# Loading q, k and v of six batches as fp32 through the hardware queue, with the cast on GpSimd or VectorE, and transposing one more batch of x by DMA

## The chip, the cores and the metric

The kernel runs on one core of a Trainium2 chip. A core has TensorE (PE, matrix multiplication; its weight loads are shown as PEld), VectorE (DVE), ScalarE (ACT), GpSimd (POOL) and SyncE (SP, which here only issues transfers), each with a program of its own that it works through in order. Engines wait for one another through semaphores. DMA engines, 16 for the core, move data between HBM and the core's memory; transfers are issued by SyncE or ScalarE (the hardware queues) or by GpSimd (the software queue). A transfer from GpSimd may change the type of the data on the way[...].

The metric is the time of one execution on the device in microseconds, the median of several runs. The profile comes from one profiled execution; its span, from the first to the last instruction, is about 2 us shorter than the time.

## What is computed

Attention with a relative position bias for 8 batches of 8 heads, 576 positions and a head size of 64, and behind it a feed-forward layer with a squared relu on all 4608 rows:

```python
batch, n_heads, seq, head_dim = (8, 8, 576, 64)          # q, k, v in fp32
scores = scale * np.matmul(q, k.transpose(0, 1, 3, 2))
bias = bias_table[bucket]                                # depends on |i - j| only
scores = scores + bias.transpose(2, 0, 1)[None, :, :, :]
attn = np.exp(scores - np.max(scores, axis=-1, keepdims=True))
attn = attn / (np.sum(attn, axis=-1, keepdims=True) + 1e-09)
attn_out = np.matmul(attn, v)

x = attn_out.transpose(0, 2, 1, 3).reshape(B * S, H * D)  # 4608 x 512
h = np.maximum(x @ w_in, 0.0)                             # w_in  512 x 2048
out = h * h @ w_out                                       # w_out 2048 x 512, out in fp32
```

## The kernel before

Everything is computed in fp16 with sums in fp32. The kernel describes its work as operations with an estimated length, the buffers they hold, what they depend on and when they are due. A planner in the program sorts them into an order for every engine; the chip then runs these fixed orders. Constants such as `LEAD`, `PERIOD`, `G0` and `GP` set when attention and the layers are due, and so shape the order. They are no times of the chip.

The heads are worked on in pairs, four pairs per batch, 32 in all:

```python
DT_QK = 3
PERIOD, LEAD, FAST, FASTN = 9000.0, 9900.0, 4500, 6
AHEAD, G0, GP = 9800.0, 30900.0, 41900.0
DT_X = 2
RELU_DVE = 0
NSTG, NQK, NPT, NV, NX, NGB, NRT, NY = 2, 4, 2, 3, 2, 2, 4, 3   # buffers of each kind
SIX = 3
ORDER = "i0 i1 q0 k1 k0 i2 q1 o0 i3 v o1 o2 o3"                 # loads of w_in, w_out, batch 1
```

Loading. All loads of q, k, v and the weights are issued by GpSimd, in a fixed order, and turn fp32 into fp16 on the way. Batches 0 to 2 (`b < SIX`) lay q and k out in six positions per row, the others in plain rows of 64 elements:

```python
def load_six(b, w, h0, nh):
    l = load("POOL", nc.gpsimd,
        lambda: six(stg[b_stg[b].slot][w])[:, h0 : h0 + nh, :],
        const(src[b, h0 : h0 + nh].rearrange("h (p j) d -> p h (j d)", j=6)), ...)

def load_qk(b, w):                       # batches 3 to 7: ten transfers for q, ten for k
    tails = [load("POOL", nc.gpsimd, ...) for e in range(2)]
    for hp in range(4):
        l_qk[b, w, hp] = tails + [load("POOL", nc.gpsimd, ...) for e in range(2)]

def load_v(b):                           # four transfers of 128 rows, two for the last 64
    for tt in range(4):
        l = load("POOL", nc.gpsimd,
            lambda tt=tt: vas[b_v[b].slot][:, tt, :, 0:64],
            const(v[b, :, ts(tt, 128), :].transpose([1, 0, 2])), ...)
    load_v_tail(b)
```

Attention of a pair. q and k are transposed, by TensorE for batches 0 to 2 and by DMA from SyncE for the others (`b >= DT_QK`), asked for 6 us ahead of the scores. The last 64 positions of the two heads are copied into a small zeroed tile (`spread`). Scores (`L622`) use half of TensorE's rows for each head. Exponentials follow on ScalarE (`L633`, `L656`, `L681`), products with the bias factors on VectorE (`L714`), multiplication with v on TensorE (`L752`, `L759`), and division by the row sum on VectorE (`L776`, `L781`). The last two steps are done in two halves that share one PSUM buffer:

```python
if b >= DT_QK:
    nc.sync.dma_start_transpose(out=dst[qb.slot]..., in_=rows(stg[...][w])[:, hp]...)
elif b < SIX:                            # L577: 12 small transposes of 96 rows each
    for j in range(6):
        for e in range(2):
            nc.tensor.transpose(ps[ds(64 * e, 64), ts(j, 96)], six(t)[:, 2 * hp + e, ts(j, D)], id_sb[0:96, 0:96])
else:                                    # 5 transposes of 128 columns
    for j in range(5):
        nc.tensor.transpose(ps[:, ts(j, 128)], rows(t)[:, hp, j, :], id_sb)

def sp(o, ...):                          # L604, on VectorE or GpSimd
    eng.tensor_copy(out=dst[qb.slot][rw, rw], in_=src[qb.slot][rw, 512:576])

for part, qt0, nq in ((0, 0, 3), (1, 3, 2)):
    bank = Buf(r_pv)                     # one PSUM buffer
    ...                                  # L752, L759, then L776 and L781 on VectorE
    if b >= DT_X:                        # x transposed by DMA (L797), else by TensorE (L819)
        nc.sync.dma_start_transpose(out=xt_sb[:, hp, c : c + 128 * nq]..., in_=xs[xb.slot][...]...)
```

The layers. `xt_sb` is a ring for four batches of x (`XB = 4`, 2304 columns). The 4608 rows are done in nine groups of 512. Group g's first layer (`L914`, 16 blocks of 128 outputs, 4 matmuls each) is laid beside group g-1's second layer (`L864`). A group that runs over the end of the ring takes two matmuls in place of one:

```python
n = min(GT, XR - c)
for a, z, c in ((0, n, c), (n, GT, 0)):
    for kk in range(4 if z > a else 0):
        nc.tensor.matmul(g_ps[bank.slot][:, a:z], w_in_sb[:, kk, ts(nt, 128)], xt_sb[:, kk, c : c + z - a], ...)
...
engs = {"ACT": act(512), "DVE": dve(512)} if g < RELU_DVE else {"ACT": act(512)}   # L935, relu
nc.vector.tensor_tensor(out=gs[gb1.slot][:, nt, :], in0=rts[rb.slot], in1=rts[rb.slot], op=MULT)   # L945
```

Of the kernel before, what the change touches and what calls it, by code (L numbers as in the profile page):

```python
# [10 lines left out]
FP32 = mybir.dt.float32  # L11
FP16 = mybir.dt.float16
# [5 lines left out]
B, H, S, D = 8, 8, 576, 64  # L18
# [6 lines left out]
VW = 66  # L25
GT = 512
NG = B * S // GT
XB = 4
XR = XB * S
DT_QK = 3  # L30
PERIOD, LEAD, FAST, FASTN = 9000.0, 9900.0, 4500, 6
AHEAD, G0, GP = 9800.0, 30900.0, 41900.0
DT_X = 2
RELU_DVE = 0
NSTG, NQK, NPT, NV, NX, NGB, NRT, NY = 2, 4, 2, 3, 2, 2, 4, 3
SIX = 3
ORDER = "i0 i1 q0 k1 k0 i2 q1 o0 i3 v o1 o2 o3"


def _bucket(n):  # L40
# [140 lines left out]
def kernel(  # L181
# [10 lines left out]
    nc = tc.nc  # L192
    assert (_bucket(np.arange(128, S)) == NBK - 1).all()

    def io(ins):
        tc.keep_in_program_order(ins)
        return ins
# [10 lines left out]
    def sb(name, shape, dtype=FP16):  # L208
        return single.tile(shape, dtype, name=name)
# [3 lines left out]
    w_out_sb = sb("w_out_sb", [128, 16, 512])  # L213
# [8 lines left out]
    stg = [[sb(f"{n}s{i}", [128, 6 * 512]) for n in "qk"] for i in range(NSTG)]  # L222
# [7 lines left out]
    vas = [sb(f"va{i}", [128, 4, H, VW]) for i in range(NV)]  # L230
    v4s = [sb(f"vm{i}", [128, 4, 2, VW]) for i in range(NV)]
    xs = [sb(f"x{i}", [128, 4, 5, 128]) for i in range(NX)]
    xt_sb = sb("xt", [128, 4, XR + 64])
    gs = [sb(f"g{i}", [128, 16, GT]) for i in range(NGB)]
    rts = [sb(f"rt{i}", [128, GT]) for i in range(NRT)]
    ys = [sb(f"y{i}", [128, 512], FP32) for i in range(NY)]
    rs = [sb(f"r{i}", [128, 3, 2, 1], FP32) for i in range(2)]
# [4 lines left out]

    P = Plan()
    r_set, r_pv, r_g, r_lane = Ring(2), Ring(1), Ring(3), Ring(8)
    r_stg, r_qk, r_pt, r_v, r_x = Ring(NSTG), Ring(NQK), Ring(NPT), Ring(NV), Ring(NX)
    r_gb, r_rt, r_y, r_r = Ring(NGB), Ring(NRT), Ring(NY), Ring(2)

# [14 lines left out]
    def one_of(engs, fn, deps, bufs, due):  # L262
        op = P.add(engs, None, deps, bufs, due)
        op.fn = lambda: fn(op)
        return op

    def const(f):
        return lambda: f

    def load(eng_name, eng, out_, in_, packets, deps=(), bufs=(), due=0.0):  # L270
        return loader(eng_name, eng, out_, in_, packets, deps, bufs, due)[0]
# [30 lines left out]
        for i in range(4)  # L302
# [11 lines left out]
                out=eb_sb, in0=sel_sb, in1=ex_sb.rearrange("p (a h) -> p a h", a=1).to_broadcast([128, 4, 8]), op=MULT  # L314
# [43 lines left out]
    first, z_fix = [], []  # L358
# [37 lines left out]
    l_qk = {}  # L396
# [3 lines left out]
    def pdue():  # L400
        pool_due[0] += 1.0
        return pool_due[0]
# [5 lines left out]
    def rows(t):  # L408
        return t[:, 0:2560].rearrange("p (c t d) -> p c t d", c=4, t=5)

    def load_six(b, w, h0, nh):
        src = (q, k)[w]
        l = load(
            "POOL", nc.gpsimd,
            lambda: six(stg[b_stg[b].slot][w])[:, h0 : h0 + nh, :],
            const(src[b, h0 : h0 + nh].rearrange("h (p j) d -> p h (j d)", j=6)),
            96 * nh * 75, (), [b_stg[b]], pdue(),
        )
        for hp in range(h0 // 2, (h0 + nh) // 2):
            l_qk[b, w, hp] = [l]  # L420

    def load_qk(b, w):
        src = (q, k)[w]
        tails = [
            load(
                "POOL", nc.gpsimd,
                lambda e=e: rows(stg[b_stg[b].slot][w])[0:64, :, 4, ds(64 * e, D)],
                const(src[b, e::2, 512:S, :].transpose([1, 0, 2])),
                256 * 34.5, first, [b_stg[b]], pdue(),
            )  # L430
            for e in range(2)
        ]
        for hp in range(4):
            l_qk[b, w, hp] = tails + [
                load(
                    "POOL", nc.gpsimd,
                    lambda hp=hp, e=e: rows(stg[b_stg[b].slot][w])[:, hp, 0:4, ds(64 * e, D)],
                    const(src[b, 2 * hp + e, 0:512, :].rearrange("(t p) d -> p t d", p=128)),
                    512 * 34.5, first, [b_stg[b]], pdue(),
                )  # L440
                for e in range(2)
            ]

    def load_v_head(b, h):
        l = load(
# [16 lines left out]
                l_v.setdefault((b, hp), []).append(l)  # L462

    def load_v(b):
        for tt in range(4):
            l = load(
                "POOL", nc.gpsimd,
                lambda tt=tt: vas[b_v[b].slot][:, tt, :, 0:64],
                const(v[b, :, ts(tt, 128), :].transpose([1, 0, 2])),
                1024 * 34.5, v_all, [b_v[b]], pdue(),  # L470
            )
            for hp in range(4):
                l_v.setdefault((b, hp), []).append(l)
        load_v_tail(b)
# [34 lines left out]
    for step in ORDER.split():  # L509
        if step[0] == "i":  # L510
            load_w_in(int(step[1]))
        elif step[0] == "o":
            load_w_out(int(step[1]))
        elif step[0] in "qk":
            load_six(1, "qk".index(step[0]), 4 * int(step[1]), 4)
        else:
            load_v(1)
    for b in range(2, B):
        for w in range(2):
            if b < SIX:  # L520
                load_six(b, w, 0, 8)
            else:
                load_qk(b, w)
        load_v(b)


# [478 lines left out]
```

The softmax here doesn't subtract the row's maximum and nothing guards it: scores larger than these inputs give would overflow.

## Time and profile before

| | |
|---|---|
| time, median of 3 runs | 388.77 us (388.37 to 389.11) |
| span of the profiled execution | 386.6 us |
| TensorE busy | 370.2 us |
| ScalarE busy | 261.0 us |
| VectorE busy | 202.6 us |
| GpSimd busy, with the making of descriptors | 151.5 us |
| packets of the software queue | 94,432, 59.8% of 16 engines' span |
| packets of the hardware queue | 49,488, 24.2% of 16 engines' span |
| granted clock of TensorE | full throughout |

How to read it: a group's line gives the busy time of its instructions together, their mean length, and behind a second bar the idle time of their engine just before them with what ended it. Lengths of matmuls overlap, as they are pipelined; where the cost of one counts, the distance from one start to the next is what to take. The chain that ended last follows the run back from its last instruction, at each step to what released it. A share of the DMA engines over 1 in a stretch means that packets overlapped.

### The profile page before, as it was taken

To read this page: it belongs to the slowest core of one execution; us is meant where nothing else is said; L and a number is where in the kernel's file an instruction comes from. 1 tells how busy PE (TensorE), PEld (TensorE's weight loads), DVE (VectorE), ACT (ScalarE), POOL (GpSimd) and SP (SyncE) were. 2 spreads that over 40 slices of the span, in tenths; PEclk is the share of its full clock that TensorE was granted. 3 is DMA by queue.
4 is the path that set the end of the run, shared out by engine and by line. 5 is a ranking of instruction groups with operands and counts; after the bars stand their busy time and mean duration, and the time that the engine had idled before them with its cause. 6 is when DMAs were issued, how large, how long until landed. Compare 5 with 4: busy or idle time off the path is not lost.

```text
span 386.6 us, 8896 instructions
## 1 busy us (share of the span) xinstructions
PE 370.2 (96%) x3544; PEld 200.4 (52%) x3544; DVE 202.6 (52%) x526; ACT 261.0 (68%) x372; POOL 151.5 (39%) x260
## 2 busy tenths in 40 slices
PE   2779999999999999999999999999999999999996
PEld 2547455754445545454567665455544545444444
DVE  5889664856644654466545464545456442432200
ACT  2798986979766885689676675857478652654421
POOL 8884720595527364725338452835420000000000
PEclk9999999999999999999999999999999999999999
DMA  7999996499769598989989799799950112001012
GB/s 101 151 194 192 147 192 67 53 109 143 81 115 115 95 127 116 134 104 113 97 126 90 82 114 171 84 87 131 163 88 27 36 66 80 27 0 49 35 54 83
DMA packets 144201, 39.04 MB, mean 101 GB/s; under 512 B 130592, under 2 KB 139680, under 8 KB 144160
## 3 DMA queue, kind: packets, MB, share of 16 engines
q0 software_dynamic: 94432, 18.36, 59.8%
q1 hardware_dynamic: 49488, 19.98, 24.2%
q8 instruction: 28, 0.46, 0.5%
q10 hardware_dynamic: 240, 0.13, 0.2%
q14 instruction: 13, 0.11, 0.1%
HBM read 36.87 MB, written 9.44 MB: 120 GB/s over the span
## 4 chain that ended last, share of the span: by engine, by line
PE 89%; DMA 4%; ACT 3%; DVE 2%; issue 1%; SPq 0%; ACTq 0%; DVEq 0%
PE f L914 33%; PE f L864 30%; PE pv L759 9%; PE st L622 8%; PE pv L752 3%; PE st L671 2%; PE f L577 2%; PE st L646 2%; ACT pt L633 2%; DMA kt<-ks 1%; DMA xt<-x 1%; DMA far_sb<-in_bias_table_dram 1%; PE f L819 1%; ACT pt L656 0%; DVE pt L714 0%
## 5 line engine op out<-in xcount | busy, mean ns | idle before, releaser
L633 ACT ACTIVATE pt<-st 128x1024 f16<-128x1024 f32 x128 | 126.8, 1022 | 36.9 <-PE st L622 36.8
L864 PE MATMUL f<-w_out_sb,g 128*128 128x512 f16 (+1 forms) x592 | 141.0, 373 | 0.0
L914 PE MATMUL f<-xt,w_in_sb 128*128 128x512 f16 (+1 forms) x640 | 140.4, 358 | 0.1
L935 ACT ACTIVATE rt<-f 128x512 f16<-128x512 f32 x144 | 85.5, 598 | 48.5 <-PE f L914 47.2
L945 DVE TENSOR_TENSOR g<-rt 128x512 f16<-128x512 f16 x144 | 60.8, 422 | 66.6 <-ACT rt L935 65.8
L914 PEld LDWEIGHTS <-w_in_sb 128*128 128x128 f16 x640 | 59.1, 98 | 62.0 <-issue 10.6
L864 PEld LDWEIGHTS <-g 128*128 128x128 f16 x592 | 54.7, 98 | 57.7 <-issue 5.9
L714 DVE TENSOR_TENSOR pt<-pt,tb_sb 128x512 f16<-128x512 f16 (+2 forms) x96 | 59.0, 623 | 26.9 <-ACT pt L633 26.7
L759 PE MATMUL pv<-va,pt 128*128 128x65 f16 x1280 | 54.6, 193 | 0.0
L759 PEld LDWEIGHTS <-pt 128*128 128x128 f16 x1280 | 50.2, 97 | 4.3 <-issue 0.3
L604 POOL COPY qz<-qt 64x64 f16<-64x64 f16 x44 | 12.6, 286 | 85.7 <-DMA qt<-qs 56.9
L255 POOL DMA_DIRECT2D qs<-in_q_dram x57 | 40.8, 729 | 5.2 <-PE f L914 2.3
L622 PE MATMUL st<-qt,kt 64*128 64x512 f16 x256 | 40.1, 385 | 2.8 <-ACT pt L633 1.2
L255 POOL DMA_DIRECT2D ks<-in_k_dram x57 | 40.9, 747 | 1.8 <-issue 1.1
L752 PE MATMUL pv<-vm,pm 128*128 128x130 f16 x160 | 35.4, 221 | 0.3 <-DVE x L781 0.3
L781 DVE TENSOR_TENSOR x<-pv,r 128x384 f16<-128x384 f32 x64 | 31.4, 490 | 1.8
L255 POOL DMA_DIRECT2D va<-in_v_dram x36 | 30.8, 872 | 0.7 <-DMA ks<-in_k_dram 0.4
L776 DVE RECIPROCAL r<-pv 128x6 f32<-128x6 f32 x64 | 11.9, 187 | 36.0 <-PE pv L759 35.9
L604 POOL COPY kz<-kt 64x64 f16<-64x64 f16 x38 | 12.4, 327 | 39.7 <-DMA kt<-ks 35.9
L884 ACT ACTIVATE y<-f 128x512 f32<-128x512 f32 (+1 forms) x19 | 11.0, 578 | 21.0 <-PE f L864 20.8
L681 ACT ACTIVATE pm<-st 128x576 f16<-128x576 f32 x32 | 20.9, 652 | 4.2 <-PE st L671 4.0
L656 ACT ACTIVATE pt<-st 128x512 f16<-128x512 f32 x32 | 19.2, 600 | 3.6 <-PE st L646 3.4
(49 smaller groups left out, 174.7 us busy)
## 6 DMA issues: line engine op xcount, KB each, us to landing
out_dram<-y SPq DMA_DIRECT2D x35, 256.0 KB, 2.3
va<-in_v_dram POOLq DMA_DIRECT2D x28, 128.0 KB, 5.6
qs<-in_q_dram POOLq DMA_DIRECT2D x40, 64.0 KB, 3.1
ks<-in_k_dram POOLq DMA_DIRECT2D x40, 64.0 KB, 3.3
w_in_sb<-in_moe_w_in_dram POOLq DMA_DIRECT2D x4, 512.0 KB, 9.6
w_out_sb<-in_moe_w_out_dram POOLq DMA_DIRECT2D x4, 512.0 KB, 8.4
xt<-x SPq DMA_TRANSPOSE x48, 3.2
qs<-in_q_dram POOLq DMA_DIRECT2D x4, 144.0 KB, 4.8
```

The source lines that it names most:

```text
L255: lambda: io(eng.dma_start(out=out_(), in_=in_())),
L604: io(eng.tensor_copy(out=dst[qb.slot][rw, rw], in_=src[qb.slot][rw, 512:576]))
L622: nc.tensor.matmul(sets_ps[st.slot][:, e, :], kt[rw, ts(jt, 128)], qt[rw, 0:512], start=True, stop=True,)
L633: nc.scalar.activation(out=p5(pts[pb.slot])[:, jt, :, 0:512], in_=sets_ps[st.slot], func=EXPF, scale=SCALE)
L714: io(nc.vector.tensor_tensor(out=a, in0=a, in1=t, op=MULT))
L752: nc.tensor.matmul(ps[:, i, :, :], pm[:, c : c + 128], vm[:, hp, :, 0:65], start=True, stop=False)
L759: nc.tensor.matmul(ps[:, i, e, :], pt[:, (2 * jt + e) * S + c : (2 * jt + e) * S + c + 128], va[:, jt, 2 * hp + e, 0:65], start=False, sto ...
L781: nc.vector.tensor_tensor(out=xs[xb.slot][:, hp, qt0 : qt0 + nq, :].rearrange("p t (e d) -> p t e d", e=2), in0=ps[:, :, :, 0:64], in1=rs[ ...
L864: nc.tensor.matmul(g_ps[bank.slot][:, 0:cn], gs[gb.slot][:, nt, ts(m, 128)], w_out_sb[:, nt, c0 : c0 + cn], start=(nt == 0), stop=(nt == 15),)
L914: nc.tensor.matmul(g_ps[bank.slot][:, a:z], w_in_sb[:, kk, ts(nt, 128)], xt_sb[:, kk, c : c + z - a], start=(kk == 0), stop=(kk == 3),)
L935: io(nc.scalar.activation(out=rts[rb.slot], in_=g_ps[bank.slot], func=RELUF))
L945: nc.vector.tensor_tensor(out=gs[gb1.slot][:, nt, :], in0=rts[rb.slot], in1=rts[rb.slot], op=MULT)
```

## The change

q, k and v of batches 2 to 7 no longer come through GpSimd's transfers. SyncE loads tiles of 128 rows and 8 heads as fp32 into six buffers, and GpSimd or VectorE, whichever the planner picks, casts each into its place. The first of these loads is held back by a tiny transfer that reads w_out's second block, and so waits for it: batch 2 is not to take bandwidth from the weights. That frees GpSimd of most of its descriptors. Batch 2 now has plain rows (`SIX = 2`), so its q and k are transposed in five pieces. x of batch 1 is transposed by DMA (`DT_X = 1`). To make room for the buffers, the ring of x holds three batches. For the first three groups the relu may run on VectorE, the order of the first loads is another, and the constants of the planner are set anew.

```diff
-XB = 4
+XB = 3
-PERIOD, LEAD, FAST, FASTN = 9000.0, 9900.0, 4500, 6
-AHEAD, G0, GP = 9800.0, 30900.0, 41900.0
-DT_X = 2
-RELU_DVE = 0
+PERIOD, LEAD, FAST, FASTN = 8700.0, 4200.0, 4500, 6
+AHEAD, G0, GP = 7800.0, 24000.0, 41200.0
+DT_X = 1
+RELU_DVE = 3
-SIX = 3
-ORDER = "i0 i1 q0 k1 k0 i2 q1 o0 i3 v o1 o2 o3"
+NF = 6
+FOLLOW = 1
+SIX = 2
+ORDER = "i0 k0 q0 i1 q1 i2 k1 v o0 o1 i3 o2 o3"
...
+    fs = [sb(f"f32{i}", [128, 512], FP32) for i in range(NF)]
...
+    def through(src, put, n, w, dst_buf, engs, deps):
+        fb = Buf(r_f)
+        f32 = lambda: fs[fb.slot].rearrange("p (h d) -> p h d", d=D)
+        deps0 = []
+        if not started:
+            deps0 = [P.add({"SP": 430.0}, lambda: io(nc.sync.dma_start(
+                out=fs[fb.slot][0:1, 0:8].bitcast(FP16), in_=w_out_sb[0:1, 4 * FOLLOW + 3, 0:16])),
+                [l_wout[FOLLOW]], [fb], pdue())]
+            ...
+        issue = P.add({"SP": 430.0}, lambda: io(nc.sync.dma_start(out=f32()[n], in_=src)), deps0, [fb], pdue())
+        t = P.add({"DMA": w * 22.2 / 16}, None, [issue], [fb], pool_due[0])
+        def cast(o):
+            for out_, in_ in put(f32()):
+                io((nc.vector if o.eng == "DVE" else nc.gpsimd).tensor_copy(out=out_, in_=in_))
+        return one_of(engs, cast, [t] + list(deps), [fb, dst_buf], pool_due[0])
...
     def load_qk(b, w):
-        tails = [load("POOL", nc.gpsimd, ...) for e in range(2)]
+        ls = []
+        for tt in range(5):
+            n = 128 if tt < 4 else 64
+            ls.append(through(src[b, :, ds(128 * tt, n), :].transpose([1, 0, 2]), ...,
+                              {"POOL": 760.0, "DVE": 370.0}, first))
...
     def load_v(b):
+        if b >= SIX:
+            ls = [through(v[b, :, ts(tt, 128), :].transpose([1, 0, 2]), ..., {"POOL": 760.0, "DVE": 370.0}, v_all)
+                  for tt in range(4)]
+            for e in range(2):
+                ls.append(through(v[b, e::2, 512:S, :].transpose([1, 0, 2]), ..., {"POOL": 380.0, "DVE": 300.0}, v_all))
...
     for b in range(2, B):
         for w in range(2):
-            if b < SIX:
-                load_six(b, w, 0, 8)
-            else:
-                load_qk(b, w)
+            load_qk(b, w)
         load_v(b)
```

## The prediction

> **What bounds the kernel now.** I read the busy times first, then busy times by stretch, then the chain of work that ended last, the groups of instructions, and last the queues.
>
> ```profile
> PE 370.2 (96%) x3544; PEld 200.4 (52%) x3544; DVE 202.6 (52%) x526; ACT 261.0 (68%) x372; POOL 151.5 (39%) x260
> ...
> DMA  7999996499769598989989799799950112001012
> ...
> PE 89%; DMA 4%; ACT 3%; DVE 2%; issue 1%; SPq 0%; ACTq 0%; DVEq 0%
> ```
>
> TensorE is busy for 370.2 of 386.6 us and makes 89% of the last chain; the next engine, ScalarE, has 68%. The DMA engines are full too for the first 300 us (digits of 9), so the question is whether TensorE ever waits for them. Five stretches chosen at the places where TensorE's behaviour changes answer that (stretch, its length, then busy time of PE, PEld, DVE, ACT, POOL, and the DMA share):
>
> ```profile
> 0.00:5.30 5.30, 0.00 (x0) 0.00 (x1) 3.32 (x31) 1.28 (x1) 4.22 (x11) 1.00 0.43 62
> 5.30:27.00 21.70, 15.77 (x317) 11.20 (x318) 15.95 (x38) 16.15 (x23) 19.17 (x32) 1.00 1.37 165
> 27.00:40.30 13.30, 11.70 (x249) 8.71 (x246) 11.77 (x30) 11.91 (x18) 6.29 (x16) 1.00 1.54 186
> 40.30:383.00 342.70, 342.52 (x2990) 180.44 (x2984) 171.52 (x427) 231.24 (x332) 121.83 (x204) 1.00 0.80 95
> 383.00:386.60 3.60, 0.22 (x2) 0.00 (x0) 0.00 (x0) 0.38 (x1) 0.00 (x0) 1.00 0.17 59
> ```
>
> All of TensorE's 16.4 us of idle time is at the ends: 5.3 before the first q has landed, 5.9 up to 27 us, 1.6 up to 40.3, 3.4 behind the last matmul. From 40.3 us, when the feed-forward layers have their first x, it is idle for 0.18 us out of 342.7. Loads, GpSimd and the DMA engines are busy there, and hidden. So only three things can move the end: fewer TensorE instructions, less idle time in the first 40 us, or new idle time in the middle.
>
> **What the Trainium skill says.** Four places bear on this.
> - "DMA: Bandwidth & Descriptors", Queues, rings and completion order: each issuing queue has its own ring on each of the 16 DMA engines, which take turns between rings at packet granularity. Two rings share here; after the change loads and transposes stand behind one another in one. The trace of before shows two queues at work (lines below), not the order within a ring.
> - "GPSIMD Engine Reference", 3.1 Elementwise: a one-input loop of 512 elements takes 769 ns on GpSimd. No run here shows that size yet; the 64-element copy takes 237 ns.
> - "SBUF — State Buffer", Who interferes with whom: GpSimd and VectorE share a port pair as an exclusive lock, and a VectorE instruction with two SBUF inputs blocks a GpSimd instruction that reads SBUF. The trace agrees in sign: the same GpSimd copy takes 231 to 2113 ns (line below).
> - "Trainium Kernel Development and Optimization", Reading a trace: matmul busy time is a bad measure of distance to the roofline. I therefore price TensorE work by the spacing of instructions, not by busy share.
>
> **The change part by part.** The order of instructions on TensorE can be compared without running anything. For the first 324 matmuls (to 28.1 us in the trace of before) it is the same in both kernels.
>
> (a) TensorE's work. The groups concerned, with their mean durations, and two stretches of the chain (start, length, what):
>
> ```profile
> L577 PE MATMUL f<-id_sb,qs 96*64 96x96 f16 x144 | 5.6, 216 | 5.3 <-DMA qs<-in_q_dram 5.3
> L819 PE MATMUL f<-id_sb,x 128*128 128x128 f16 x40 | 3.1, 219 | 0.0
> ...
> 205.05 0.87 PE f L914 x8
> ...
> 329.65 12.95 PE f L914 x60
> ```
>
> The means (216, 219 ns) contain the pipeline's latency; spacing is what counts. In order of time, 12 of the small transposes at 30.12 us end where the next group starts, at 30.50: 0.38 us for 12. Eight of the 128-column ones run from 38.44 to 38.88: 0.055 us each. Batch 2 leaves the small form: 8 sets of 12 (8 x 0.38 = 3.0 us) become 8 sets of 5 large ones (40 x 0.055 = 2.2 us): -0.8 us. The x of batch 1 leaves TensorE: 20 of the 40 x transposes, -1.1 us. The smaller ring for x (3 batches, not 4) wraps inside two groups of 512 rows instead of one; a wrapped set of four takes 8 halves, 0.87 us as at 205.05, against 4 x 12.95/60 = 0.86 us; 16 more sets cost 0.2 us. Attention and the other layer matmuls keep their counts. Sum: **-1.7 us**, nearly all in the full stretch, so on the path.
>
> (b) The start. The first layer matmul moves up behind two score sets of batch 1 rather than one, batch 1's k and q are loaded ahead of w_in's second block, and the weights w_in 3 and w_out later. None of this can touch the first 27 us. Of the 1.6 us idle up to 40.3, some is a wait for k of batch 1 and for a bank (0.61 us at 33.86) and some is ScalarE being late. I take **-1.0 us**, out of a possible -1.6. That the weights come later costs nothing by my count: w_in blocks take about 4 us each to land behind one another in the trace, and w_in 3 then lands near 47 us, while its first use is 48 layer matmuls (10.4 us) and some 6 us of attention after the start of the layers, near 56.
>
> (c) GpSimd and VectorE. Of 174 DMA issues on GpSimd, 0.64 to 0.87 us each, 36 stay (26 us at 0.73). In place of the others it has 60 casts: an estimate from the skill's 0.77 us for 54 of them, and 0.4 for the six small ones of v's last rows, is 44 us. With 84 copies at 0.3 GpSimd falls from 151.5 to about 95 us. VectorE gains 36 casts (estimate 0.4 us: a 128x576 fp16 copy takes 0.75 out of PSUM, and this one reads SBUF), 20 relu at 0.69 (the row of the y copy), and loses 8 y copies and 6 x copies: about +21 us, to 224. ScalarE loses 20 x 0.60 and gains 8 x 0.60 and a little: about 254. None of them comes near TensorE's 370.
>
> (d) DMA. The rows of the queues:
>
> ```profile
> q0 software_dynamic: 94432, 18.36, 59.8%
> q1 hardware_dynamic: 49488, 19.98, 24.2%
> ...
> L604 POOL COPY kz<-kt x38: 231/237/2113, 21.3 to 288.7; 64x64 f16<-64x64 f16 x38
> ...
> DMA to landing us min/median/max: 2.3/3.2/6.0
> ```
>
> A software packet costs 0.598 x 16 x 386.6 / 94432 = 39 ns, a hardware one 0.242 x 16 x 386.6 / 49488 = 30 ns. Some 75,000 packets leave the first queue (47 points of share), and 6 x 3 x 4608 = 82,944 rows of 256 bytes enter the second at an estimated 30 ns (40 points): the sum falls from 84% to about 77%. That is hidden time, as TensorE does not wait for it now.
>
> (e) New waits. SyncE issues 96 loads, 96 transposes and 37 stores in one order. A load has to wait until one of six buffers has been cast, and everything behind it waits too. A transpose of q, k or x now stands behind loads in the same ring; a load of 1024 rows is 64 packets per engine, 64 x 30 ns = 1.9 us. Transposes land 3.2 us after issue in the median now, 6.0 at most, and the code asks for q and k 6 us ahead of their scores. A delay of one or two loads is covered, one of four is not. I put the mean at **+0.5 us** with a long tail.
>
> Sum: 388.8 - 1.7 - 1.0 + 0.5 = 386.6; I say 386.5.
>
> **Rivals.**
> 1. The single queue becomes the bound: loads held up by buffers, transposes by loads, so TensorE waits at scores or at the first layer of a group. For it: SyncE's order mixes them tightly, with about 26 us of issue per batch of 42 us (16 loads at an assumed 0.4, 16 transposes at 1.2, the store's 0.4 four or five times), and the critical chain already passes through a k transpose (1.5%) and an x transpose (1.3%). Against it: GpSimd's queue is no longer full and the DMA share falls. Eight batches with 1 us lost in each would make 394, with 2 us 400.
> 2. Casts on GpSimd hold the shared port, so VectorE's products and normalisations come late. There is one PSUM buffer for the attention output, so a late normalisation stops TensorE. For it: the 2113 ns copy shows that the two do block each other. Against it: in before TensorE waited only 0.3 us for the normalisation in the whole run. If a third of the 64 later halves lost 0.15 us each, +3 us: 389.5.
> 3. The start gains more than I think, because the layers fill ScalarE-bound time sooner. The ceiling is the 1.6 us idle plus perhaps 1 us of slow spacing: 384.
>
> **Range and chances.** Without any new wait the kernel lands between 384 and 387; with rival 2, or rival 1 in weak form, between 388 and 391. Range 383.8 to 391.0. A gain of over 2% needs 381.0, that is 7.8 us, while work and removable idle time give at most 1.7 + 1.6 and some spacing: 0.03. A loss over 2% needs 396.5, nearly 10 us of new waits, rival 1 in strong form: 0.10. Within 2%: 0.87.
>
> **What would show it.** TensorE's instructions fall by 12 matmuls net, and its busy time with the same start by about 2 us; idle time from 40 us on stays under 1 us if I am right; a row of TensorE waits for a DMA of qt, kt or xt shows rival 1, waits for x or pt from VectorE with GpSimd copies above 1 us show rival 2. GpSimd should read about 95 us, the software queue about 12%, the hardware queue about 64%. A TensorE idle of several us in the middle, or a start of the layers earlier than 38 us, would make the prediction wrong.

## The result and the profile after

The changed kernel takes 402.26 us (400.96 to 404.17) against 388.80 (388.37 to 389.11) for the kernel before on the same chip: 1.035 times as long, interval 1.031 to 1.040. The profiled execution spans 400.0 us against 386.6.

The page of the changed kernel, with the rows that answer to those of before: busy times of the engines, the DMA engines in forty slices, the two queues (packets, MB, share), and the last chain by engine.

```profile
PE 374.5 (94%) x3532; PEld 205.6 (51%) x3532; DVE 223.9 (56%) x568; ACT 254.5 (64%) x359; POOL 97.0 (24%) x184
...
DMA  8999977899779989988997987233211120010112
...
q1 hardware_dynamic: 136816, 41.87, 50.2%
q0 software_dynamic: 16960, 7.74, 15.4%
...
PE 77%; DVE 11%; DMA 7%; ACT 2%; issue 1%; SPq 1%; POOL 0%; DVEq 0%; ACTq 0%; POOLq 0%
```

GpSimd falls from 151.5 to 97.0 us and the DMA engines have more room, as intended. But TensorE's share of the last chain falls from 89% to 77%, and VectorE (11%, was 2%) and transfers (7%, was 4%) take its place. TensorE has new holes. Where they are is seen in the changed kernel's busy times by stretch (stretch, its length, busy time of PE, PEld, DVE, ACT, POOL, then TensorE's clock, the DMA share and GB/s):

```profile
5.30:27.00 21.70, 16.56 (x302) 11.45 (x302) 15.22 (x36) 15.22 (x21) 18.66 (x31) 0.92 1.37 164
27.00:40.30 13.30, 12.26 (x258) 8.97 (x256) 11.68 (x32) 12.38 (x17) 7.73 (x18) 1.00 1.26 133
40.30:100.00 59.70, 59.05 (x526) 31.03 (x524) 45.77 (x108) 40.83 (x58) 13.05 (x25) 1.00 0.94 181
100.00:150.00 50.00, 47.19 (x441) 24.14 (x438) 34.15 (x82) 34.41 (x46) 15.97 (x31) 1.00 0.84 173
150.00:200.00 50.00, 45.94 (x498) 29.19 (x496) 27.66 (x70) 37.05 (x51) 16.24 (x32) 1.00 0.96 164
200.00:250.00 50.00, 46.85 (x419) 24.34 (x420) 30.31 (x77) 32.41 (x46) 18.29 (x28) 0.93 0.87 179
250.00:300.00 50.00, 50.00 (x473) 27.05 (x472) 28.77 (x74) 37.06 (x53) 2.79 (x10) 1.00 0.27 64
```

Length less busy is idle: 0.65, 2.81, 4.06 and 3.15 us in the four stretches from 40.3 to 250 us, 10.7 in all, where before had 0.18 from 40.3 on. It ends when the loads end: from 250 us on the DMA share drops to 0.27 and TensorE is full. The clock column has a second loss: 0.93 of full speed from 200 to 250 us, 0.92 from 5.3 to 27. The trace shows three windows of 3.41 us at half clock, at 17.0, 201.4 and 232.1 us. By an estimate each costs half its length, 1.7 us.

The sum, as span after less span before: idle to 40.3 us 11.48 against 12.83, -1.35; idle behind 40.3 us +10.5; tail 3.34 against 3.38, 0; busy time 374.5 against 370.2, +4.3. Of the last, the predicted saving of work is -1.7, so +6.0 has to be explained; the half clock gives 3 x 1.7 = 5.1, and 0.9 stays open. Together +13.4.

Who stopped TensorE, and who stopped the one that did, is in the changed kernel's waits (engine and line, what ended the wait: us in total, times, longest):

```profile
DVE kz L661 <- DMA kt<-ks: 23.8, 11, 6.2
...
DVE qz L661 <- DMA qt<-qs: 8.7, 5, 3.3
...
PE pv L816 <- DVE pt L771: 7.2, 4, 3.9
```

VectorE stands 32.5 us in front of the 64 x 64 copies of `spread` (L661, L604 in before), waiting for a k or q transposed by DMA; in before these waits come to 6.4 us:

```profile
DVE kz L604 <- DMA kt<-ks: 3.3, 3, 1.6
DVE qz L604 <- DMA qt<-qs: 3.1, 3, 1.4
```

TensorE's own largest new wait is for VectorE's product with the bias (L771), 7.2 us in four pieces. One of the four, followed through the timeline of VectorE and then of TensorE (start, length, what; in brackets the idle time ahead and what ended it):

```profile
192.25 0.42 DVE L838 TENSOR_TENSOR x<-pv,r 128x256 f16<-128x256 f32 x1
198.88 0.23 DVE L661 COPY kz<-kt 64x64 f16<-64x64 f16 x1 [6.21 <-DMA kt<-ks]
199.14 0.77 DVE L300 CAST qs<-f 64x512 f16<-64x512 f32 x1
199.83 0.94 DVE L771 TENSOR_TENSOR pt<-pt,tb_sb 128x1536 f16<-128x1536 f16 x1
```

```profile
196.75 0.19 PE L816 MATMUL pv<-va,pt 128*128 128x65 f16 x1
200.83 0.39 PE L816 MATMUL pv<-va,pt 128*128 128x65 f16 x7 [3.88 <-DVE pt L771]
```

VectorE had other work, the product at L771, but it works in order and a copy whose k was not there stood ahead of it. TensorE ran out of work at 196.9 us and stood for 3.88. At 201.4 the first late window at half clock begins.

Why was k not there? SyncE's timeline in the changed kernel (L295 is a load, L617 a transpose of q or k, L854 one of x):

```profile
185.08 4.64 SPq L295 DMA_DIRECT2D f<-in_q_dram  x2
189.81 1.25 SPq L854 DMA_TRANSPOSE xt<-x  x1
191.15 0.53 SPq L295 DMA_DIRECT2D f<-in_k_dram  x1
191.78 1.22 SPq L617 DMA_TRANSPOSE qt<-qs  x1
193.09 0.53 SPq L295 DMA_DIRECT2D f<-in_k_dram  x1
193.67 1.27 SPq L617 DMA_TRANSPOSE kt<-ks  x1
195.04 2.58 SPq L295 DMA_DIRECT2D f<-in_k_dram  x2
```

and in the kernel before at the same time (L560 q or k, L797 x):

```profile
180.56 1.20 SPq L560 DMA_TRANSPOSE qt<-qs  x1
181.94 1.20 SPq L560 DMA_TRANSPOSE kt<-ks  x1
186.44 1.18 SPq L797 DMA_TRANSPOSE xt<-x  x1
187.78 1.20 SPq L560 DMA_TRANSPOSE kt<-ks  x1
```

Before, there is air between the issues: 3.3 us without any from 181.94 + 1.20 to 186.44, in less than 9 us. After, from 189.10 on, each one starts less than 0.2 us behind the last. The pair at 185.08 is two loads with 3.49 us between them, from 185.61 to 189.10: the second waits for a buffer, and all behind it wait too. GpSimd's timeline shows who held the buffer, and the view of the casts' line how long such a cast takes (count; shortest, median, longest in ns):

```profile
185.44 0.23 POOL L661 COPY kz<-kt 64x64 f16<-64x64 f16 x1 [2.83 <-DMA kt<-ks]
185.73 3.79 POOL L300 CAST vm<-f 64x256 f16<-64x256 f32 x2
...
L300 POOL CAST vm<-f x6: 398/454/3337, 84.9 to 252.9; 64x256 f16<-64x256 f32 x6
```

The first of these two casts took 3.34 us, seven times the median, and ended at 189.07; VectorE was busy without a pause until 188.8. That would fit the lock of rival 2, but no run here separates it from other causes. The cast had itself stood behind a copy that waited for k. So in this stretch the delay feeds itself: late transposes hold up GpSimd's copies, these its casts, the casts the buffers, and the buffers the queue of the next transposes.

Adding the lengths of SyncE's issues from 80 to 250 us gives 150 of 170 us, against 88 in before. The k transpose went out at 193.67 and landed at 198.8, while its data was long there. The changed kernel's view for the staging tiles of k between 150 and 194 us (count; shortest, median, longest in ns; first to last start):

```profile
L617 SPq DMA_TRANSPOSE kt<-ks x5: 1217/1273/1848, 148.7 to 193.7; - x5
L300 DVE CAST ks<-f x3: 416/484/495, 161.5 to 172.3; 128x512 f16<-128x512 f32 x3
L300 POOL CAST ks<-f x2: 607/608/609, 161.1 to 171.2; 128x512 f16<-128x512 f32 x1, 64x512 f16<-64x512 f32 x1
```

The last cast into k's staging tiles starts at 172.3 us, 21 us ahead of that transpose. The transposes themselves are as quick as before in the median: 3.3 to 3.4 us from issue to landing against 3.4 to 3.6. (This one took 5.1, so 1.8 us of its lateness lies behind the issue.) What changed is when they go out. Where VectorE makes the copy, a k transpose was issued 4.4 us in the median before VectorE came to that copy in before, and 2.5 us in the changed kernel; for q it is 4.7 and 3.0. In before that covers a landing, after it does not. None of this shows in a busy row, as issuing is not counted there.

### The profile page after: what moved, and what is told of

It is laid out like the page before. It is cut to its first block, busy times and chain, and to the rows that moved or that the text cites. A ratio compares the mean times of both kernels' runs of the same rounds, so it can differ in the third digit from the quotient of the medians.

```text
span 400.0 us, 8968 instructions
## 1 busy us (share of the span) xinstructions
PE 374.5 (94%) x3532; PEld 205.6 (51%) x3532; DVE 223.9 (56%) x568; ACT 254.5 (64%) x359; POOL 97.0 (24%) x184
## 3 DMA queue, kind: packets, MB, share of 16 engines
q1 hardware_dynamic: 136816, 41.87, 50.2%
q0 software_dynamic: 16960, 7.74, 15.4%
## 4 chain that ended last, share of the span: by engine, by line
PE 77%; DVE 11%; DMA 7%; ACT 2%; issue 1%; SPq 1%; POOL 0%; DVEq 0%; ACTq 0%; POOLq 0%
PE f L921 29%; PE f L971 27%; PE pv L816 8%; PE st L679 7%; DMA kt<-ks 4%; DVE pt L771 3%; DMA qt<-qs 3%; PE pv L809 2%; DVE g L1002 2%; DVE rt L994 1%; PE st L728 1%; ACT pt L690 1%; PE st L703 1%; DMA far_sb<-in_bias_table_dram 1%; DVE x L838 1%
## 5 line engine op out<-in xcount | busy, mean ns | idle before, releaser
L971 PE MATMUL f<-xt,w_in_sb 128*128 128x512 f16 (+4 forms) x704 | 145.0, 342 | 1.8 <-DVE rt L994 1.7
L992 ACT ACTIVATE rt<-f 128x512 f16<-128x512 f32 x124 | 73.9, 598 | 57.4 <-PE f L971 55.8
L1002 DVE TENSOR_TENSOR g<-rt 128x512 f16<-128x512 f16 x144 | 63.7, 445 | 62.1 <-ACT rt L992 61.1
L971 PEld LDWEIGHTS <-w_in_sb 128*128 128x128 f16 x704 | 62.7, 98 | 65.2 <-issue 16.3
L771 DVE TENSOR_TENSOR pt<-pt,tb_sb 128x512 f16<-128x512 f16 (+2 forms) x96 | 62.5, 660 | 20.1 <-ACT pt L690 17.9
L661 POOL COPY qz<-qt 64x64 f16<-64x64 f16 x45 | 14.5, 325 | 87.3 <-DMA qt<-qs 45.9
L941 ACT ACTIVATE y<-f 128x512 f32<-128x512 f32 (+1 forms) x27 | 15.7, 582 | 24.3 <-PE f L921 24.0
L661 POOL COPY kz<-kt 64x64 f16<-64x64 f16 x39 | 14.8, 379 | 63.2 <-DMA kt<-ks 45.0
L300 POOL CAST qs<-f 128x512 f16<-128x512 f32 (+1 forms) x20 | 14.1, 711 | 28.2 <-DMA f<-in_q_dram 27.5
L809 PEld LDWEIGHTS <-pm 128*128 128x128 f16 x160 | 15.7, 98 | 9.2 <-issue 4.8
L661 DVE COPY kz<-kt 64x64 f16<-64x64 f16 x25 | 4.9, 196 | 24.5 <-DMA kt<-ks 23.8
```

What stands on the lines that cost most here:

```text
L661: io(eng.tensor_copy(out=dst[qb.slot][rw, rw], in_=src[qb.slot][rw, 512:576]))
L771: io(nc.vector.tensor_tensor(out=a, in0=a, in1=t, op=MULT))
L809: nc.tensor.matmul(ps[:, i, :, :], pm[:, c : c + 128], vm[:, hp, :, 0:65], start=True, stop=False)
L992: io(nc.scalar.activation(out=rts[rb.slot], in_=g_ps[bank.slot], func=RELUF))
```

## The experiments

The theory: SyncE's one ordered queue is nearly full, so transposes go out late; VectorE's ordered queue stands behind a small copy that needs one, and TensorE behind VectorE. The rivals: VectorE's and GpSimd's new casts themselves make the products late (the second rival of the prediction); the new constants of the planner are to blame; the bytes of fp32 are, and not the number of issues. Ratios are to the kernel before on the same chip. "Idle" is TensorE's from 40.3 us on (before 0.18, after 10.7); "SyncE" is the sum of its issues from 80 to 250 us (before 88, after 150). Both come from one profiled execution. With twelve buffers that was the fastest of four (393.37 us, no window at half clock), with `DT_X = 1` nearly the slowest (394.78). Five executions that fell in a slower state of the chip, 395.32 to 402.08 us of four kernels and one of the kernel before, are left out of the ratios and not of the times. Edits are to the changed kernel where nothing else is said; where an edit adds lines, the line numbers of that kernel are higher by 2.

| kernel | time, us | ratio, interval | idle | SyncE |
|---|---|---|---|---|
| changed kernel | 402.26 | 1.035 [1.031, 1.040] | 10.7 | 150 |
| copies on GpSimd | 395.04 | 1.015 [1.011, 1.020] | 6.4 | 152 |
| same, and all casts on GpSimd | 397.14 | 1.017 [1.011, 1.023] | 4.5 | 151 |
| loads issued by GpSimd | 395.21 | 1.013 [1.009, 1.017] | 7.6 | 93 |
| new loading, old constants | 396.24 | 1.017 [1.013, 1.020] | 5.1 | 145 |
| old loading, new constants | 410.11 | 1.052 [1.048, 1.056] | 16.3 | 82 |
| loads of 1 head in 8 | 391.34 | 1.004 [1.001, 1.007] | 2.4 | 138 |
| no loads | 390.89 | 1.002 [0.999, 1.004] | 2.5 | 96 |
| twelve buffers | 397.10 | 1.017 [1.011, 1.023] | 6.5 | 153 |
| twelve buffers, copies on GpSimd | 393.11 | 1.008 [1.005, 1.010] | 4.5 | 156 |

**The copies away from VectorE.** For the batches whose q and k come by DMA, GpSimd alone makes the copies of `spread`.

```diff
-                    eng = nc.vector if o.eng == "DVE" else nc.gpsimd
+                    eng = nc.vector if o.eng == "DVE" and b < DT_QK else nc.gpsimd
```

> The changed kernel with one edit: for batches 3 to 7 the 64x64 copies of the last positions of q and k always run on GpSimd, none on VectorE; every engine keeps its planned order otherwise. Theory A (VectorE's in-order queue stands still behind a copy that waits for a late q or k transpose): VectorE's waits for kt and qt fall from 32.5 us to under 3 us, the five TensorE stalls of 1 to 4 us go, TensorE idle from 40 to 250 us falls from 10.7 to under 4 us, time 388 to 396 us. Theory B (more work and port conflicts on VectorE from casts and relu) and theory C (the planner's new constants): no change, 399 to 404 us.

395.04 us. VectorE's waits for k and q are gone, and with them TensorE's wait for L771. SyncE's queue is as full as before, 152 of 170 us. TensorE's idle time is 6.4 us, where I had said under 4. What is left comes by another way, the line of TensorE's waits in this kernel:

```profile
PE f L971 <- DMA xt<-x: 4.4, 3, 2.9
```

The first layer waits for x, whose transposes stand in the same queue. So the way through VectorE is shown to cost some 7 us (ratio 1.035 to 1.015), and the late transposes cost more by a second way.

**Is it VectorE's and GpSimd's own work?** The casts go to GpSimd as well.

```diff
-                io((nc.vector if o.eng == "DVE" else nc.gpsimd).tensor_copy(out=out_, in_=in_))
+                io(nc.gpsimd.tensor_copy(out=out_, in_=in_))
```

> The changed kernel with the copies of the last positions of batches 3 to 7 and all 96 casts on GpSimd, so that VectorE's queue holds nothing that waits for a transfer, and has 36 casts less; order otherwise as planned. Theory A with SyncE's full queue as the root: what VectorE lost is gone but transposes stay late, so TensorE waits for x or k directly; 391 to 396 us, about as with the copies alone moved (395.0). If VectorE's casts and port conflicts mattered as well (theory B): under 391 us.

397.14 us, a little above what I expected and no different from 395.04 by the intervals. 36 casts fewer on VectorE bring nothing, and 36 more on GpSimd cost nothing that shows. So it is not the casts' work on either engine. Whether a cast that ends late holds up a load is another matter; the twelve buffers below bear on that.

**Which part of the change?** Two kernels split it. The first keeps the new loading and sets all constants back to those of before (four batches of x in the ring, `DT_X = 2`, `RELU_DVE = 0`, the old `ORDER`, `LEAD`, `PERIOD`, `AHEAD`, `G0`, `GP`). The second keeps the new constants and loads as before, through GpSimd; q and k of batch 2 stay in plain rows, which takes 18 transfers more.

> The new loading of batches 2 to 7 alone: ring of x, planner constants, first loads, x transposes and relu as before. Theory A: still slow, 394 to 404 us, with VectorE waiting over 10 us for kt and qt. Theory C (the constants): 386 to 390 us. Theory B puts most of its cost here too: 395 to 404 us, but without long VectorE waits for transposes.

> The changed kernel with q, k and v of batches 2 to 7 loaded as before by GpSimd with the cast in the transfer; all constants, the order of the first loads, x of batch 1 by DMA and relu on VectorE as in the changed kernel. Theory A: 385 to 391 us, SyncE's queue at about 90 of 170 us. Theory C: 398 us or more. The predicted part (a) of 1.7 us should show here if nothing else moves.

396.24 and 410.11 us. The new loading alone loses 6.5 us by the same way (VectorE waits 27 us for k and q, TensorE 4.5 us for L771). The second falsified what I expected of it, 385 to 391: the new constants ask for attention earlier (`LEAD` 4200 for 9900), the old loads do not deliver by then (SyncE's transposes wait 9.6 us for loads of q), and TensorE waits for k itself, as its waits show:

```profile
PE st L658 <- DMA kt<-ks: 9.8, 5, 3.5
```

So the constants are no tuning that can be added alone, and with the new loading as the change has it they cost as well: without them the ratio is 1.017, with them 1.035.

Old loading and old constants with only `DT_X = 1` is the smallest part of the change:

```diff
-DT_X = 2
+DT_X = 1
```

> The kernel before with x of batch 1 transposed by DMA and nothing else: 20 matmuls of 0.055 us leave TensorE. By the spacing -1.1 us, to 387 to 389 us, if no new wait appears; SyncE has room (88 of 170 us).

392.07 us, 1.007 [1.004, 1.010]. I counted on a gain of 1.1 us, the 20 transposes that TensorE no longer does; the planner's order changes with it, and 4.7 us of idle time arrive (1.6 of it waiting for x, 1.1 for k). This order had no room for the eight DMA transposes that take the place of the 20.

**Loads in another queue.** GpSimd issues the new loads in place of SyncE; everything else stays.

```diff
-        issue = P.add({"SP": 430.0}, lambda: io(nc.sync.dma_start(out=f32()[n], in_=src)), deps0, [fb], pdue())
+        issue = P.add({"SP": 430.0}, lambda: io(nc.gpsimd.dma_start(out=f32()[n], in_=src)), deps0, [fb], pdue())
```

> The changed kernel with the 96 fp32 loads issued by GpSimd in place of SyncE, in the same planned places; casts as they are. Theory A with its cause in SyncE's queue (150 of 170 us spent on issuing between 80 and 250 us): SyncE's issuing falls to about 90 of 170 us, transposes are issued earlier, VectorE waits under 10 us for kt and qt, time 388 to 396 us unless GpSimd, with 96 x 0.9 us more, becomes the late one. Theories B and C: 399 to 404 us.

395.21 us. SyncE is down to 93 of 170 us, nearly as in before, and 7 us come back, but not all. VectorE still waits 18 us for k and q, where I had said under 10: the k transposes now land 4.7 us after issue in the median (3.3 when all were in one queue), and GpSimd, with 174 us of work, is late. A queue with room is not enough when transfers from another one share the DMA engines.

**More room for the loads.** Twelve buffers in place of six, with the planned order left as it is; then the same with the copies on GpSimd.

```diff
-    fs = [sb(f"f32{i}", [128, 512], FP32) for i in range(NF)]
+    fs = [sb(f"f32{i}", [128, 512], FP32) for i in range(12)]
...
+        fb.at = len(taken) % 12
+        taken.append(fb)
```

> The changed kernel with twelve fp32 buffers in place of six, used in turn; the planned order of every engine is unchanged, so a load finds its buffer long free. Theory E (loads that wait for a cast hold SyncE's queue and all transposes behind them): loads no longer wait, VectorE's waits for kt and qt fall from 32.5 us to about 15, time 391 to 396 us. Theory D (traffic in front of the transposes): loads go out earlier still, transposes land no sooner, 400 to 405 us.

> Twelve buffers and the copies of the last positions of batches 3 to 7 on GpSimd. If theories A and E both hold, the remaining wait of the first layer for x (4.4 us with the copies alone moved) goes as well: 388 to 392 us. Under theory D about 395, as with the copies alone moved.

397.10 and 393.11 us. The buffers alone take the ratio from 1.035 to 1.017, with the copies moved to 1.008. In the changed kernel SyncE stood 3.5 us at 185.6 and 1.6 us at 236.2 with nothing issued; with twelve buffers no gap between 80 and 250 us is over 0.8. TensorE's wait for the product at VectorE falls from 7.2 to 3.5 us. But both expectations were too good: VectorE's waits for k and q fall only to 29.3 us and not to about 15, and a k transpose still goes out 2.5 us ahead of its copy. So the longest stops came in part from loads waiting for a buffer; the general lateness did not. With the copies moved as well, a wait for x of 3.5 us stays that I had expected to go, with SyncE at 156 of 170.

**Bytes or issues?** Two kernels that leave work out. In the first each load brings one of eight heads, the rest of the buffer being zero; in the second the 96 loads are left out and the casts read zeroed buffers. So q, k and v of six batches are mostly zero; every other instruction is there, with six fills of the buffers added.

> The changed kernel with each of the 96 loads cut to one head of eight (or of four): as many issues on SyncE in the same places, an eighth of the bytes and rows; buffers are zeroed once beforehand, so q, k and v of batches 2 to 7 are mostly zero and the values are not the reference's. If the number of issues on SyncE is the root: transposes are still late, 397 to 403 us. If the traffic in front of the transposes in the rings or the DMA engines is the root (theory D): 385 to 390 us.

> The changed kernel with the 96 loads left out altogether, casts kept and reading zeroed buffers (values are not the reference's): SyncE issues only transposes and stores. Both theory A and D: 384 to 388 us, TensorE idle from 40 us on under 1 us. Theory B (VectorE's added work and port conflicts, all still there): 395 us or more. The gap to the tiny loads is what the issues alone cost.

391.34 and 390.89 us. My expectation for the first on the theory of issues alone, 397 to 403, failed: with nearly all issues kept (138 of 170 us) nearly all of the loss is gone. The tiny loads land 1.9 us after issue, the transposes 2.6, so buffers come back sooner. A k transpose goes out no earlier, 2.5 us ahead of its copy, but that now nearly covers its landing. VectorE still waits 18.1 us for k and q, in pieces of at most 2.9, and TensorE is idle for 2.4 us only: what counts is not the sum of these waits, but the long ones. It is the loads with their bytes that cost, through their landing times as well as their issuing.

The second is the more telling. Its page and its stretch from 150 to 200 us:

```profile
PE 368.7 (95%) x3532; PEld 203.5 (53%) x3532; DVE 229.0 (59%) x574; ACT 254.6 (66%) x359; POOL 91.9 (24%) x184
```

```profile
150.00:200.00 50.00, 50.00 (x537) 31.29 (x536) 32.41 (x78) 38.80 (x53) 15.28 (x32) 1.00 0.36 79
```

VectorE and GpSimd do all their casts, copies and relu, VectorE more of it inside the same stretch than in the changed kernel (32.4 us against 27.7), and TensorE is full. So the casts by themselves stop nobody. A cast that frees a buffer too late, as the one of 3.34 us above, cannot show here, as no load waits for a buffer. My 384 to 388 us with under 1 us of idle time failed too: with loads that cost nothing the kernel is no faster than before. The work is 1.5 us less (368.7 against 370.2), and 2.2 us of new idle time between 40.3 and 100 us use it up.

**Which transfer has to leave SyncE's queue?** From the kernel with twelve buffers and copies on GpSimd, four more: all loads issued by ScalarE; only v's loads by ScalarE; v as in before, through GpSimd with the cast on the way; and all as it was, but planned with the measured issue times.

```diff
-        issue = P.add({"SP": 430.0}, lambda: io(nc.sync.dma_start(out=f32()[n], in_=src)), deps0, [fb], pdue())
+        issue = P.add({"SP": 430.0}, lambda: io((nc.scalar if src.tensor.name == v.tensor.name else nc.sync).dma_start(
+            out=f32()[n], in_=src)), deps0, [fb], pdue())
```

> Twelve buffers, copies on GpSimd, and all 96 loads issued by ScalarE in place of SyncE. If SyncE's issuing time is what is left: the first layer's wait for x goes, 388 to 391 us, unless ScalarE (128 of 170 us busy between 80 and 250 us, plus some 35 us of issuing) becomes late, then 394 us or more with TensorE waiting for exponentials. If the bytes are what is left: TensorE still waits for x, about 393 us.

> Twelve buffers, copies on GpSimd, and the 36 loads of v alone issued by ScalarE: some 13 us of issuing leave SyncE between 80 and 250 us. If issuing time is what is left: 389 to 392 us, TensorE's wait for x under 1.5 us. If the bytes: 393 us, wait for x about 3.5 us.

> Twelve buffers, copies on GpSimd, q and k of batches 2 to 7 by the new path, v as before by GpSimd with the cast in the transfer (36 issues and 36 casts fewer on the new path, 36 software transfers back). If SyncE's issuing is what is left: SyncE under 135 of 170 us, TensorE idle from 40 us on under 2 us, 387 to 391 us. If every new order of the plan brings waits of its own, 392 us or more.

> Twelve buffers, copies on GpSimd, and the planner told SyncE's measured issue times (0.60 for a load, 1.40 and 1.35 for transposes, in place of 0.43, 1.25 and 1.00), which gives another order. If the order drifted because SyncE was planned too fast: 388 to 391 us. If the order is not the cause: 392 to 396 us.

In that order 393.71 (1.011 [1.006, 1.016]), 392.48 (1.008 [1.005, 1.012]), 392.10 (1.008 [1.004, 1.012]) and 393.97 us (1.011 [1.006, 1.016]); none differs from 1.008 [1.005, 1.010]. But the waits differ. With v's loads by ScalarE, the bytes are the same and SyncE issues for 134 us; TensorE no longer waits for x, and in its place stand

```profile
PE st L705 <- ACT pt L715: 1.6, 1, 1.6
PE st L705 <- ACT pt L692: 1.5, 1, 1.5
```

ScalarE's exponentials. ScalarE's timeline shows what they stood behind, in the second of these waits:

```profile
161.53 1.02 ACT L692 ACTIVATE pt<-st 128x1024 f16<-128x1024 f32 x1
164.45 0.37 ACTq L297 DMA_DIRECT2D f<-in_v_dram  x1
164.93 1.02 ACT L692 ACTIVATE pt<-st 128x1024 f16<-128x1024 f32 x1 [2.38 <-issue]
```

The load's own issue is 0.37 us; it stood for nearly 2 us before. In this trace the transfers of SyncE and ScalarE share eight semaphores that tell of their landing, and one that reuses a semaphore waits for the transfer that had it. Here that was a transpose of x by SyncE, landed at 164.38. With all loads by ScalarE it is the same (2.8 us for an exponential): from 116.05 to 121.12 us a load waits for a k transpose that landed at 121.09, though SyncE is down to 96. The transposes of q and k land after some 4.5 us there. So an engine that takes the issues over takes their waits over too, and they come out near TensorE again.

For x it was SyncE's issuing time and not the bytes. Among the kernels with the copies on GpSimd, TensorE waits for x for 2.0 to 4.4 us in the six where SyncE issues for 146 to 156 us, and for 0 to 0.9 in the four where it issues for 96 to 134; two of these four move the same bytes as the six. With v through GpSimd 3.9 us of idle time are left, 2.1 of it for k. Planning with 600, 1400 and 1350 ns for a load, a q or k transpose and an x transpose, in place of 430, 1250 and 1000, was expected to give 388 to 391 and did not: these three figures alone do not make the order better.

**Versions for the best of it.** New loading, old constants and copies on GpSimd; the same with twelve buffers; and that with v as in before.

> The new loading alone with the constants of before (396.2 us, TensorE idle 5.1 us from 40 us on, VectorE waiting 27 us for kt and qt), and now the copies of the last positions of batches 3 to 7 on GpSimd. Theory A: VectorE's waits go, TensorE idle under 2 us, 388 to 392 us. Otherwise 395 us or more.

> The new loading with the constants of before, copies of batches 3 to 7 on GpSimd (394.4 us so far) and twelve buffers. Theories A and E: 388 to 391 us; theory D: 393 to 396 us.

> The same with the constants of before (ring of x, x transposes, relu, first loads, planner). SyncE under 130 of 170 us; 387 to 391 us if SyncE's queue was what held it at 395.

394.35 (1.012 [1.008, 1.017]), 395.16 (1.014 [1.010, 1.018]) and 390.68 us (1.002 [1.000, 1.005]). The first missed its 388 to 392, with 2.0 us of waiting for x, and the second its 388 to 391, with 3.4. The third, q and k by SyncE and only v left to GpSimd, is no different from before. Two of its stretches:

```profile
100.00:150.00 50.00, 50.00 (x495) 26.35 (x493) 30.02 (x71) 35.67 (x51) 18.12 (x39) 1.00 1.16 160
...
200.00:250.00 50.00, 49.21 (x552) 32.35 (x549) 29.19 (x72) 38.13 (x52) 14.65 (x34) 1.00 0.98 144
```

TensorE is full again while q and k of six batches still come through the hardware queue, with SyncE at 132. That is the loading made harmless, not made useful. No kernel tried beats the one before.

## Why the prediction was wrong

- **Step (e), new waits, +0.5 us: the step that failed.** Measured: 10.5 us more of idle time. The inputs were too low: a load was assumed at 0.4 us of SyncE's time and took 0.65 in the mean (0.53 in the median, up to 2.0); a transpose took 1.35 to 1.42, not 1.2. The "26 us of issue per batch of 42", 62%, was 88% (150 of 170), and what was left were the gaps for want of a buffer and the short pauses between issues. And what the step counted was how long a transpose stands behind loads in the ring, where the median loses nothing here (3.3 us to landing, as before); the delay is ahead of the ring, before the issue: 2.5 us ahead of the copy in place of 4.4. That a load waits for a buffer and holds up all behind it, the step did say, but it gave this no length; 3.5 us were seen. Its 3.2 us to landing was the line of x; q and k took 3.4 to 3.6 in before.
- **The way from a late transpose to TensorE was not in it.** I expected TensorE to wait for qt, kt or xt. In the changed kernel it waits for VectorE, which stands in front of a copy. A copy of 0.2 us on an engine at 52% was no suspect by any busy figure.
- **The half clock was not in it.** After the long waits, TensorE's clock was halved twice, and once early: about 5 us, which no term of the sum had.
- **Rival 1 was the right one and had too small a share.** Its "2 us" in each of eight batches, 400 us, is near what came; it was put aside because GpSimd's queue and the DMA share would relax. Both did, and neither was what TensorE waited for. It, too, had TensorE waiting for scores or x, and not for VectorE.
- **Rival 2 fell as the bound**, by the kernel with all casts on GpSimd and by the one without loads. One slow cast did play a part, in another way than the rival had it: it held a buffer, and so SyncE's queue, ahead of the longest stop. The mark that I gave it, TensorE waiting for x or pt from VectorE, did appear (7.2 and 1.5 us), but came from rival 1. It did not tell the two apart.
- **Steps (c) and (d) held, and (a) as far as it can be seen.** 12 matmuls fewer; 1.5 us less busy time without loads (with loads, in the two kernels that had no window at half clock, it is 370.3 and no less than before, so the saving does not show there). GpSimd 97.0 (said 95), VectorE 223.9 (224), ScalarE 254.5 (254). The cast of 128 x 512 took 0.61 us in the median on GpSimd, where 0.77 was the estimate from the Trainium skill, "GPSIMD Engine Reference", 3.1 Elementwise; 0.4 on VectorE was right. The software queue has 15.4% (said 12), the hardware queue 50.2% (said 64: a packet took 0.502 x 16 x 400 / 136816 = 23.5 ns, not 30).
- **Step (b) held in its sign, with about half its size.** Idle time up to 40.3 us is 1.35 less (said 1.0), but that this is near is luck: 0.8 of it lies ahead of 27 us, where the step said that nothing could change, and where the half clock at 17.0 us makes TensorE busy for longer. From 27 us on it is 1.04 against 1.60, 0.6 less, and with the copies on GpSimd, without that window, it is 1.03.

Not settled: how much of the loss is SyncE's issuing time and how much the later landing of everything behind fp32 bytes. Tiny loads speak for the bytes, the waits for x for the issuing time. Nor is it known why, under the old constants, twelve buffers bring nothing (1.014 against 1.012), when they bring 1.8 points under the new ones.

## What to carry to other kernels

Count an issuing queue as an engine: add up the lengths of its issues in the stretch that matters, with the gaps in which a load waits for a buffer or for an earlier landing, before more is put into it; the busy rows do not show it. Keep a small instruction that waits for a transfer out of the ordered queue of an engine on which the critical one depends, for it holds back all that stands behind it. And ask first what the critical engine waits for: here TensorE was idle for 0.18 us in all from 40.3 us on, so relieving GpSimd and the DMA engines there could bring nothing, and the queue that took the load over went from 88 to 150 of 170 us.

## What the hardware showed beside that

- TensorE's clock: windows of 3.41 us at half speed. The Trainium skill, "TensorE: Matmul & The Clock Gate", Part 1, says that the half rate returns after an idle window of about 3.4 us. The trace agrees for the window at 201.4 us, which follows 3.88 us of idle time; the one at 232.1 follows only 1.97 us. Over all the runs, single stops of 1.97 to 3.88 us behind the start were followed by such a window within 1 us of their end, or had it begin in their last microsecond, in 12 of 14 cases. The exceptions are a stop of 3.09 us with twelve buffers and one of 2.15 us with the loads issued by GpSimd. Shorter stops mostly were not followed by one; two pairs, of 1.26 and 1.55 us and of 1.10 and 0.96 us, were. So a stop of 2 us was followed by one in most cases, and by the estimate of 1.7 us then cost nearly twice its length. The number of windows is not the program's alone: the mean clock was 0.979 to 0.991 in the four executions of the changed kernel, and 0.990 to 1.000 in those with twelve buffers.
- A load, mostly of 1024 rows of 256 bytes, holds SyncE 0.53 us in the median and 0.65 in the mean; one of an eighth of the rows 0.52 and 0.53. The median does not go by the bytes; the mean does a little.
- A transpose of q or k by DMA lands after 3.3 us in the median when the 96 fp32 loads are in its own queue, and after 4.5 to 4.7 when ScalarE or GpSimd issues the same loads. That another queue is at work is not enough for it: in before all loads were GpSimd's, and it took 3.4 to 3.6.
